# Induced attention into a channel mix on one core: follow-up operations a step later, the gate a step earlier, and two squares in twelve on VectorE

## The chip, the core and the metric

The kernel runs on one core of one Trainium2 chip. TensorE (PE) multiplies matrices into PSUM, VectorE (DVE), ScalarE (ACT) and GpSimd (POOL) work element by element, SyncE (SP) issues the DMAs; each takes its instructions in program order and waits on the others' semaphores. The time is device microseconds of one execution.

## What is computed

The reference, cut to what matters; the four batches have 12608 tokens of 128 channels, there are 32 inducing points, and the hidden width is 1024.

```python
def mab(q, kv):
    s = scale * (q @ kv.transpose(0, 2, 1))
    a = np.exp(s - s.max(-1, keepdims=True))
    a /= a.sum(-1, keepdims=True) + 1e-09
    return a @ kv
h = mab(I, x)            # stage A: 32 points attend to all tokens
y = mab(x, h)            # stage B: every token attends to the 32 rows of h
y_prev = shift(y, 1)     # the token before
xk = mu_k * y + (1 - mu_k) * y_prev
xr = mu_r * y + (1 - mu_r) * y_prev
k = np.maximum(xk @ w_k, 0.0)
v = k * k @ w_v
out = sigmoid(xr @ w_r) * v
```

## The kernel before

**Folding.** Since y = a @ h, the kernel never makes y: it multiplies h into the weights (`combine`, once for each batch) and keeps for each group of 512 tokens a tile `R` with the transposed weights `a`, as a high part (`ah`) and a low part (`al`), both in a float32 form that PE takes at full rate.

**The main loop.** A batch has 25 groups (24 of 512 tokens, one of 320), a group four *units* of 256 hidden columns: 100 units a batch, 400 in all, one for each *step* n of the loop at L998. A step issues, in this order:

- `up` of unit n: four matmuls (L773, L775) into a PSUM tile `ps_a`, of which there are two;
- whatever was handed to `soon(n, ...)`;
- `square` of unit n: `k_t = max(ps_a, 0)` on DVE (L785), `kh = k_t²`, the high part, on ACT (L786), `k_t = k_t²` on ACT in place (L787), then on POOL `kl = k_t - kh` (L789); `k_t`, `kh`, `kl` have four buffers each;
- in one unit of each group, `zgate`: two matmuls (L762, L763) into the group's PSUM tile `ps_v` and the sigmoid on ACT into `rT` (L765);
- for a group finished five steps earlier, `gate` on DVE (`oT = ps_v * rT`, L805; steps with n mod 4 = 0), and a step later `store` (a transpose into `ot` on DVE, L816, and after every fourth group four DMAs on SP, L823);
- `down` of unit n-4: six matmuls (L800) that add into `ps_v`; the first overwrites the gate's logits, so it waits for the sigmoid;
- whatever was handed to `at(n, ...)`, in the order in which it was handed over.

`ps_v` has two buffers, so `zgate` of group g writes where group g-2 was, which `gate` of that group reads in step 4g.

**Segments.** Stage A of the next batch and stage B of this one run inside the loop, one block of 2048 tokens of each for every 12 steps (`SEG`, L976). Below, *position* p is the step's place in its segment, 0 to 11; a unit's number in its group is p mod 4. There are six segments a batch; the fourth batch has no stage A. Then follow `combine` and the first block of stage B of the next batch. In the first batch all begins at step 4.

What the segment begun at s issues, by position (a stage A block goes on into the next segment):

| position | stage A | stage B |
|---|---|---|
| 11, 0, 1, 3 | `btr`: transposes to `xs` (L333), four DMAs each | |
| 1 | | `scores` into PSUM bank `pb_b` (L610) |
| 2, 3 | | transpose, maximum (L617, L620); `sub` (L623) |
| 4 | `expo` of the block before (L393, L394) | `expo` (L627) |
| 5 | `etrans` of the block before (L405) | |
| 6, 7 | `hmm`: products with `e` (L426) | sums (L631); `mult`, `back` (L638, L644) |
| 8 | `acc` | `high`: `ah` out of `pb_b` on ACT (L650) |
| 9 | `scores` into bank `pb_a`, maximum (L361, L364) | `low`: `al` out of `pb_b` on DVE (L654) |
| 10 | `common`: one product into bank `pb_b` (L371) | `spread` of a group: four DMAs into `R` (L664) |
| 11 | `running`: the new maximum (L377 to L382) | `spread`, and so on until position 1 |

Each of the banks `pb_a` and `pb_b` is one buffer: who writes it next waits for its last reader. The last full block of a batch takes the 320 tokens of the tail with it (`t_tr`, `t_scores`, `t_etrans`), which shifts `common` and `running` by a step. `halo` copies the last column of one `R` into the next. `xs` has three buffers, `ot` one.

Of the kernel before, what the change touches and what calls it, by code (L numbers as in the profile page):

```python
# [12 lines left out]
AF = mybir.ActivationFunctionType  # L13
ALU = mybir.AluOpType
# [5 lines left out]
def kernel(  # L20
# [11 lines left out]
    nc = tc.nc  # L32
# [13 lines left out]
    NU = FC // UC  # L46
# [16 lines left out]
    def pb_tile(bank=None):  # L63

        return pb.tile([P, G], F32, name="pb_" + (bank or next(banks)))
# [248 lines left out]
    def stage_a(b, j, at, t):  # L314
# [8 lines left out]
        tail = j == NBLK - 2  # L323
# [122 lines left out]
            at(t + (-1, 0, 1, 3)[c], lambda c=c: btr(c))  # L446
        if tail:
            at(t + 5, t_tr)
            at(t + 10, t_scores)
        at(t + 9, scores)  # L450
        at(t + 10 + tail, common)
        at(t + 11 + tail, running)
        at(t + 16, expo)
        at(t + 17, etrans)
        if tail:
            at(t + 17, t_etrans)
# [5 lines left out]
        k = order_a.index((b, j))  # L462
# [119 lines left out]
    def halo(S, g, far=True):  # L582

        if g == 0:
            nc.vector.memset(S.R[g].bitcast(F32)[:, 0:1], 0.0)
        elif far:
            nc.sync.dma_start(out=S.R[g].bitcast(F32)[:, 0:1], in_=S.R[g - 1].bitcast(F32)[:, G:G + 1])
        else:
            nc.vector.tensor_copy(out=S.R[g][:, 0:1], in_=S.R[g - 1].bitcast(F32)[:, G:G + 1])


    def stage_b(b, j, at, t):

        S = batches[b]
        full = j < NBLK - 1
        L = {}
        if full:
            w = G  # L600
        else:
            w = (TAIL // Q + 31) // 32 * 32
            offs = [min(i * w, TAIL - w) for i in range(Q)]
        nk = w // 32

        def scores():
            ps = L["ps"] = pb_tile("b")
            for i in range(Q):
                rhs = S.xt[j, i] if full else S.xt_tail[:, offs[i]:offs[i] + w]
                nc.tensor.matmul(out=ps[M * i:M * (i + 1), :w], lhsT=S.hT, rhs=rhs,  # L610
                                 start=True, stop=True)
            for i in range(Q):
                S.xt.pop((j, i))

        def trans():
            L["s2"] = st.tile([P, Q * Q, M], F32, name="s2")[:, :nk, :]
            nc.vector.transpose(out=L["s2"].rearrange("p k m -> p (k m)"), in_=L["ps"][:, :w])  # L617

        def maxi():
            nc.vector.tensor_reduce(out=L["ps"][:, :nk], in_=L["s2"], op=ALU.max, axis=AX.X)  # L620

        def sub():
            nc.vector.tensor_tensor(out=L["s2"], in0=L["s2"], op=ALU.subtract,  # L623
                                    in1=L["ps"][:, :nk].unsqueeze(2).broadcast_to([P, nk, M]))

        def expo():
            nc.scalar.activation(out=L["s2"], in_=L["s2"], func=AF.Exp, scale=scale)  # L627

        def total():
            L["sm"] = sm.tile([P, Q * Q, 2], F32, name="sm3", bufs=1)[:, :nk, 0]  # L630
            nc.vector.tensor_reduce(out=L["sm"], in_=L["s2"], op=ALU.add, axis=AX.X)  # L631
            nc.vector.tensor_scalar(out=L["sm"], in0=L["sm"], scalar1=EPS, scalar2=None, op0=ALU.add)

        def recip():
            nc.vector.reciprocal(out=L["ps"][:, :nk], in_=L["sm"])

        def mult():
            nc.vector.tensor_tensor(out=L["s2"], in0=L["s2"], op=ALU.mult,  # L638
                                    in1=L["ps"][:, :nk].unsqueeze(2).broadcast_to([P, nk, M]))

        def back():
            L["aT"] = L["ps"][:, :w]
            if full and b > 0:
                nc.vector.transpose(out=L["aT"].rearrange("p (q s) -> p s q", q=M), in_=L["s2"])  # L644
            else:
                nc.vector.transpose(out=L["aT"], in_=L["s2"].rearrange("p k m -> p (k m)"))

        def high():
            L["ah"] = st.tile([P, G], F32R, name="ah")[:, :w]
            nc.scalar.copy(out=L["ah"], in_=L["aT"])  # L650

        def low():
            L["al"] = st.tile([P, G], F32R, name="al")[:, :w]
            nc.vector.tensor_tensor(out=L["al"], in0=L["aT"], in1=L["ah"].bitcast(F32), op=ALU.subtract)  # L654

        def spread(i):
            src = (L["ah"].bitcast(F32), L["al"].bitcast(F32))
            if full or i == 0:
                S.R[j * Q + i] = r_pool.tile([P, G + 1], F32R, name="R")
                halo(S, j * Q + i)  # L660
            R = S.R[j * Q + (i if full else 0)].bitcast(F32)
            o, lo = (0, 0) if full else (offs[i], i * w - offs[i])
            for q in range(Q):
                nc.sync.dma_start(out=R[M * q:M * (q + 1), 1 + o + lo:1 + o + w],  # L664
                                  in_=src[q % 2][M * i:M * (i + 1), lo:w])

        at(t, scores)
        at(t + 1, trans)
        at(t + 1, maxi)
        at(t + 2, sub)  # L670
        at(t + 3, expo)
        at(t + 5, total)
        at(t + 5, recip)
        at(t + 6, mult)
        at(t + 6, back)
        at(t + 7, high)
        at(t + 8, low)
        for i in range(Q):
            at(t + 9 + i, lambda i=i: spread(i))

    def stage_b_head(gs):

# [64 lines left out]
    class Group:  # L747
# [28 lines left out]
                                 start=False, stop=True)  # L776
            self.ps = ps

        def square(self, u):

            w = self.w
            k = mp.tile([P, UC * G], F32, name="k_t", bufs=4).rearrange("p (c t) -> p c t", c=UC)[:, :, :w]
            kh = mp.tile([P, UC, G], F32R, name="kh", bufs=4)[:, :, :w]
            kl = mp.tile([P, UC, G], F32R, name="kl", bufs=4)[:, :, :w]
            nc.vector.tensor_scalar(out=k, in0=self.ps[:, :, :w], scalar1=0.0, scalar2=None, op0=ALU.max)  # L785
            nc.scalar.activation(out=kh, in_=k, func=AF.Square)  # L786
            nc.scalar.activation(out=k, in_=k, func=AF.Square)  # L787
            self.h[u] = (kh, kl)
            return lambda eng, a, z: eng.tensor_tensor(out=kl[:, :, a:z], in0=k[:, :, a:z],  # L789
                                                       in1=kh.bitcast(F32)[:, :, a:z], op=ALU.subtract)  # L790
# [39 lines left out]
    def run(th):  # L830
        for f in th:
            f()
# [99 lines left out]
    def at(n, f):  # L932
        events.setdefault(n, []).append(f)

    def soon(n, f):
        early.setdefault(n, []).append(f)
# [37 lines left out]
        at(4, lambda: units[0][0].zgate(first=True))  # L974

    SEG = 12  # L976
    for b in range(B):
        t = b * UB + (4 if b == 0 else 0)
        for j in range(NBLK - 1):
            s = t + SEG * j  # L980
            if b + 1 < B:
                stage_a(b + 1, j, at, s)
            stage_b(b, j + 1, at, s + 1)
        if b + 1 < B:
            s = t + SEG * (NBLK - 1)
            combine(b + 1, at, s)
            stage_b(b + 1, 0, at, s + 13)
    units = []
    for b in range(B):
        for g in range(NG):  # L990
            grp = Group(b, g)
# [3 lines left out]
    with tc.manual_schedule():  # L995
        head()
        start()
        for n in range(len(units) + LAG + 2):  # L998
            grp, u = units[n] if n < len(units) else (None, n % NU)
            old, ou = units[n - LAG] if LAG <= n < len(units) + LAG else (None, 0)  # L1000
            if grp is None:
                run(late)
                late = []
            else:
                grp.up(u)
                run(early.pop(n, []))
                low = grp.square(u)
                run(late)
                late = []
                part = grp.w - (grp.w // 2 if n >= len(units) - 3 else 0)  # L1010
                low(nc.gpsimd, 0, part)
                if part < grp.w:
                    late = [lambda low=low, a=part, z=grp.w: low(nc.vector, a, z)]
                if n == end:
                    run(late)
                    late = []
                if n >= NU and u == 2:
                    grp.zgate()
                if u == NU - 2 and n + 2 < len(units):
                    nxt = units[n + 2][0]  # L1020
                    if nxt.b == 0 and nxt.g < Q:
                        halo(nxt.S, nxt.g, far=False)
            m = n - LAG - 1
            if 0 <= m < len(units) and units[m][1] == NU - 1:
                units[m][0].gate()
            if 1 <= m <= len(units) and units[m - 1][1] == NU - 1:
                units[m - 1][0].store()
            if old is not None:
                old.down(ou)
            run(events.pop(n, []))  # L1030
# [30 lines left out]
```

## Time and profile before

| | us |
|---|---|
| median of 3 runs | 1231.35 (1230.76 to 1233.29) |
| the profiled execution | 1226.32 |
| its span, first to last instruction | 1224.5 |
| from the first step to 361.0 (batch 1) | 305.5, PE busy 280.1 |
| 361.0 to 663.0 (batch 2) | 302.0, PE busy 285.5 |
| 663.0 to 955.0 (batch 3) | 292.0, PE busy 274.6 |
| 955.0 to the end (batch 4, no stage A) | 269.5, PE busy 253.3 |

A row of the timeline has the start in microseconds from the span's start, the duration, the engine, the line, the operation, the tiles as out<-in, the shape, and how many instructions were merged; in brackets stands the idle time of the engine before it and what ended that. A row of the waits has the waiting engine and line, what it waited for, the sum, the number of times and the longest. A matmul's duration overlaps the next one's start, so the distance of two starts is what counts.

### The profile page before, as it was taken

Reading aid. Unit: us, or ns where it says so; the run is one execution under the profiler, and the core shown is the slowest. Engines: PE = TensorE matmul, PEld = TensorE weight load, DVE = VectorE, ACT = ScalarE, POOL = GpSimd, SP = SyncE. Lnnn points to the kernel's source line nnn. Section 1 sums busy time; section 2 is a strip of 40 time slices with the busy share of each in tenths; the row PEclk is TensorE's granted clock in tenths of the full one; section 3 lists DMA queues with packets and bytes.
Section 4 is the critical chain, followed back from the end, with each engine's and each line's share of the span. In section 5 each row is a group of like instructions: output and inputs, shape, how many; then the busy total and the mean of one; then the engine's idle time right before and its main releaser. Section 6 shows DMA issues by size and latency. Waiting matters only on the chain.

```text
span 1224.5 us, 17466 instructions
## 1 busy us (share of the span) xinstructions
PE 1132.5 (92%) x5746; PEld 848.7 (69%) x5746; DVE 875.1 (71%) x1211; ACT 1030.6 (84%) x1155; POOL 949.0 (78%) x413
## 2 busy tenths in 40 slices
PE   7779999899999999998999999999899999999998
PEld 5456676667677666776678666667677777777786
DVE  5777777776777787776677777687676766766665
ACT  5478898888888888887888888898888888888996
POOL 1168877787778878886788887788778888888997
PEclk9989999999999999999999999999999999999999
DMA  9112554533326455454035353563232313322222
GB/s 277 44 45 70 128 112 104 115 96 68 51 48 128 115 116 97 107 127 97 2 76 95 99 111 101 125 126 78 40 49 53 57 28 68 70 51 54 40 37 39
DMA packets 273515, 102.30 MB, mean 84 GB/s; under 512 B 232817, under 2 KB 248337, under 8 KB 271121
## 3 DMA queue, kind: packets, MB, share of 16 engines
q1 hardware_dynamic: 273088, 101.17, 38.6%
q8 instruction: 46, 0.75, 0.3%
q14 instruction: 45, 0.36, 0.1%
q10 hardware_dynamic: 336, 0.02, 0.0%
HBM read 28.07 MB, written 25.82 MB: 44 GB/s over the span
## 4 chain that ended last, share of the span: by engine, by line
PE 66%; ACT 16%; DVE 7%; issue 5%; DMA 3%; SPq 2%; POOL 0%; DVEq 0%; ACTq 0%; POOLq 0%
PE ps_v L800 34%; PE ps_a L773 12%; PE ps_a L775 11%; ACT kh L786 5%; ACT k_t L787 3%; DVE k_t L785 3%; ACT L765 2%; PE pb_b L610 2%; PE ps_v L762 1%; PE ps_v L763 1%; PE pb_a L361 1%; ACT L393 1%; ACT rT L765 1%; ACT e1t L394 1%; DMA out_dram<-ot 1%
## 5 line engine op out<-in xcount | busy, mean ns | idle before, releaser
L789 POOL TENSOR_TENSOR kl<-k_t,kh 128x1024 fp32r<-128x1024 f32 (+2 forms) x400 | 940.3, 2367 | 228.0 <-ACT k_t L787 168.8
L785 DVE TENSOR_SCALAR k_t<-ps_a 128x1024 f32<-128x1024 f32 (+1 forms) x400 | 480.7, 1202 | 262.0 <-PE ps_a L775 243.8
L786 ACT ACTIVATE kh<-k_t 128x1024 fp32r<-128x1024 f32 (+1 forms) x400 | 417.6, 1044 | 137.0 <-PE ps_v L800 86.5
L787 ACT ACTIVATE k_t<-k_t 128x1024 f32<-128x1024 f32 (+1 forms) x400 | 419.3, 1048 | 12.7
L773 PE MATMUL ps_a<-R,W 128*128 128x512 f32 (+1 forms) x800 | 333.3, 417 | 0.7 <-ACT R L738 0.7
L775 PE MATMUL ps_a<-R,W 128*128 128x512 f32 (+1 forms) x800 | 319.5, 400 | 0.0
L800 PE MATMUL ps_v<-kh,wvh 128*128 128x512 f32 (+1 forms) x800 | 256.0, 402 | 31.3 <-ACT rT L765 31.3
L800 PE MATMUL ps_v<-kh,wvl 128*128 128x512 f32 (+1 forms) x800 | 252.2, 397 | 0.0
L800 PE MATMUL ps_v<-kl,wvh 128*128 128x512 f32 (+1 forms) x800 | 250.7, 395 | 0.0
L773 PEld LDWEIGHTS ps_a<-R,W 128*128 128x128 f32 x800 | 154.0, 193 | 75.7 <-issue 21.4
L800 PEld LDWEIGHTS ps_v<-kh,wvh 128*128 128x128 f32 x800 | 151.6, 193 | 76.2 <-ACT rT L765 42.6
L800 PEld LDWEIGHTS ps_v<-kh,wvl 128*128 128x128 f32 x800 | 153.1, 192 | 35.6
L775 PEld LDWEIGHTS ps_a<-R,W 128*128 128x128 f32 x800 | 154.7, 193 | 30.7
L800 PEld LDWEIGHTS ps_v<-kl,wvh 128*128 128x128 f32 x800 | 151.3, 190 | 35.1
L816 DVE STREAM_TRANSPOSE ot<-oT 128x512 f32<-128x512 f32 x96 | 67.2, 700 | 12.9 <-DMA out_dram<-ot 12.9
L805 DVE TENSOR_TENSOR oT<-ps_v,rT 128x512 f32<-128x512 f32 (+1 forms) x100 | 67.0, 670 | 0.6 <-PE ps_v L800 0.6
L765 ACT ACTIVATE rT<-ps_v 128x512 f32<-128x512 f32 (+1 forms) x99 | 57.2, 578 | 0.3
L333 DVE STREAM_TRANSPOSE xs<-xb 128x512 f32<-128x512 f32 x72 | 50.0, 694 | 3.1 <-DMA xt<-xs 2.6
L765 ACT ACT_TABLE_LOAD x31 | 39.8, 1283 | 0.6
L762 PE MATMUL ps_v<-R,W 128*128 128x512 f32 (+1 forms) x99 | 39.4, 398 | 0.0
L763 PE MATMUL ps_v<-R,W 128*128 128x512 f32 (+1 forms) x99 | 39.3, 397 | 0.0
L426 PE MATMUL pb_a<-xb,e 128*32 128x128 f32 x576 | 23.3, 279 | 11.7 <-DVE e L405 11.6
(193 smaller groups left out, 613.9 us busy)
## 6 DMA issues: line engine op xcount, KB each, us to landing
out_dram<-ot SPq DMA_DIRECT2D x92, 256.0 KB, 4.4
xb<-in_x_dram SPq DMA_DIRECT2D x18, 1024.0 KB, 5.1
xt<-xs SPq DMA_DIRECT2D x288, 64.0 KB, 2.0
R<-ah SPq DMA_DIRECT2D x184, 64.0 KB, 2.0
R<-al SPq DMA_DIRECT2D x184, 64.0 KB, 2.0
kh<-in_x_dram SPq DMA_DIRECT2D x4, 512.0 KB, 8.0
kl<-in_x_dram SPq DMA_DIRECT2D x4, 512.0 KB, 7.5
xb<-in_x_dram SPq DMA_DIRECT2D x8, 256.0 KB, 5.6
```

The costliest lines, as they stand in the source:

```text
L762: nc.tensor.matmul(out=ps[:, :w], lhsT=S.W[0][:, F:WF], rhs=R[:, 1:w + 1], start=True, stop=False)
L763: nc.tensor.matmul(out=ps[:, :w], lhsT=S.W[1][:, F:WF], rhs=R[:, 0:w], start=False, stop=True)
L765: nc.scalar.activation(out=self.rT, in_=ps[:, :w], func=AF.Sigmoid)
L773: nc.tensor.matmul(out=ps[:, c, :w], lhsT=S.W[0][:, cs], rhs=R[:, 1:w + 1], start=True, stop=False)
L775: nc.tensor.matmul(out=ps[:, c, :w], lhsT=S.W[1][:, cs], rhs=R[:, 0:w], start=False, stop=True)
L785: nc.vector.tensor_scalar(out=k, in0=self.ps[:, :, :w], scalar1=0.0, scalar2=None, op0=ALU.max)
L786: nc.scalar.activation(out=kh, in_=k, func=AF.Square)
L787: nc.scalar.activation(out=k, in_=k, func=AF.Square)
L789: return lambda eng, a, z: eng.tensor_tensor(out=kl[:, :, a:z], in0=k[:, :, a:z], in1=kh.bitcast(F32)[:, :, a:z], op=ALU.subtract)
L800: nc.tensor.matmul(out=self.v, lhsT=wt[:, fc, :], rhs=kk[:, c, :], start=(fc == 0 and n == 0), stop=(fc == FC - 1 and n == 2))
L805: nc.vector.tensor_tensor(out=self.oT, in0=self.v, in1=self.rT, op=ALU.mult)
L816: nc.vector.transpose(out=ot[:, o:o + w], in_=self.oT)
```

## The change

`kh` of the units at positions 4 and 10 is made on DVE, out of PSUM, right behind `k_t`. `low` and the four `spread`s of stage B come a step later. `common`, and the tail's `t_scores`, go from the end of step t+10 to the next step, behind its `up`. Stage A's `expo` comes a step earlier (position 3 of the next segment) with `etrans` where it was. `zgate` is issued with unit 1 of its group and not with unit 2, at positions 1, 5 and 9.

```diff
         if tail:
             at(t + 5, t_tr)
-            at(t + 10, t_scores)
+            soon(t + 11, t_scores)
         at(t + 9, scores)
-        at(t + 10 + tail, common)
+        soon(t + 11 + tail, common)
         at(t + 11 + tail, running)
-        at(t + 16, expo)
+        at(t + 15, expo)
         at(t + 17, etrans)
...
         at(t + 7, high)
-        at(t + 8, low)
+        at(t + 9, low)
         for i in range(Q):
-            at(t + 9 + i, lambda i=i: spread(i))
+            at(t + 10 + i, lambda i=i: spread(i))
...
-        def square(self, u):
+        def square(self, u, on_vector):
...
             nc.vector.tensor_scalar(out=k, in0=self.ps[:, :, :w], scalar1=0.0, scalar2=None, op0=ALU.max)
-            nc.scalar.activation(out=kh, in_=k, func=AF.Square)
+            if on_vector:
+                nc.vector.scalar_tensor_tensor(out=kh, in0=self.ps[:, :, :w], scalar=0.0, in1=k,
+                                               op0=ALU.max, op1=ALU.mult)
+            else:
+                nc.scalar.activation(out=kh, in_=k, func=AF.Square)
             nc.scalar.activation(out=k, in_=k, func=AF.Square)
...
     SEG = 12
+    high_vector = set()
...
             s = t + SEG * j
+            high_vector |= {s + 4, s + 10}
...
-                low = grp.square(u)
+                low = grp.square(u, n in high_vector)
...
-                if n >= NU and u == 2:
+                if n >= NU and u == 1:
                     grp.zgate()
```

Stage B is issued with t = s + 1, so its t + 9 is position 10.

## The prediction

> **What bounds the kernel now.** I read the engines' busy times first, then PE's rows in the waits, then the timeline of one ordinary segment, step by step.
>
> ```profile
> PE 1132.5 (92%) x5746; PEld 848.7 (69%) x5746; DVE 875.1 (71%) x1211; ACT 1030.6 (84%) x1155; POOL 949.0 (78%) x413
> PE ps_v L800 <- ACT rT L765: 31.3, 24, 2.2
> PE pb_a L426 <- DVE e L405: 11.6, 8, 3.3
> PE pb_b L409 <- ACT s L398: 7.6, 3, 2.5
> PE pb_a L341 <- ACT e1t L394: 6.6, 3, 2.2
> DVE ot L816 <- DMA out_dram<-ot: 12.9, 4, 4.8
> ```
>
> PE is the bound. It stands still for few things, all of which end in something late on ACT: the sigmoid, or one of stage A's exponentials (the first, second, third and fourth PE row). An ordinary step of ten matmuls takes 2.34 us (in the rows further down, starts at 807.35 and 809.70).
>
> ```profile
> 808.64 1.06 ACT L787 ACTIVATE k_t<-k_t 128x1024 f32<-128x1024 f32 x1
> 812.06 1.28 ACT L393 ACT_TABLE_LOAD   x1
> 814.22 0.62 ACT L627 ACTIVATE s<-s 128x512 f32<-128x512 f32 x1
> 818.93 1.28 ACT L765 ACT_TABLE_LOAD   x1
> 820.23 0.60 ACT L765 ACTIVATE rT<-ps_v 128x512 f32<-128x512 f32 x1
> 819.57 0.40 PE L775 MATMUL ps_a<-R,W 128*128 128x512 f32 x1
> 820.88 0.73 PE L800 MATMUL ps_v<-kh,wvh 128*128 128x512 f32 x2 [0.91 <-ACT rT L765]
> 271.15 0.63 PE L773 MATMUL ps_a<-R,W 128*128 128x512 f32 x1
> 351.84 0.73 PE L800 MATMUL ps_v<-kh,wvh 128*128 128x512 f32 x2 [2.10 <-ACT rT L765]
> 1073.55 0.63 PE L773 MATMUL ps_a<-R,W 128*128 128x512 f32 x1
> 1073.97 0.63 PE L775 MATMUL ps_a<-R,W 128*128 128x512 f32 x1
> 1077.28 0.40 PE L773 MATMUL ps_a<-R,W 128*128 128x512 f32 x1
> 1106.04 0.73 PE L800 MATMUL ps_v<-kh,wvh 128*128 128x512 f32 x2 [1.80 <-ACT rT L765]
> ```
>
> Behind the exponentials of position 4 ACT still has the squares of units 5 and 6 and a table load before the sigmoid of position 6, which ends at 820.83; at position 8 `down` needs it. The matmul of 820.88 could have started 0.23 behind that of 819.57: 1.08 late, and its pair takes 0.73 where others take 0.63. So 0.91 us shown as idle cost 1.18: to each wait of PE I add 0.27.
>
> The long waits cost twice: from 1073.55, behind a wait of 1.77, matmuls start 0.43 apart, and the step takes 3.73 and not 2.34. Such a slow stretch follows ten of the eleven waits for the sigmoid of 1.77 and above (the first at 351.84, the last at 1106.04) and none of the short ones like that of 820.88. I charge 1.4 each.
>
> [...]
>
> **What goes.** (a) The sigmoid. `zgate` at position 5 puts it ahead of the squares of unit 6; stage A's exponentials (2.16 us, from the table load at 812.06 to 814.22) are a step earlier, and unit 4's `kh` is gone from ACT. I follow ACT through: the squares of unit 3 end at 809.7 (808.64 + 1.06) and, shifted by the 0.17 of (e), near 809.9, stage A's exponentials at 812.0, the in-place square of unit 4 at 813.1, stage B's at 813.6, unit 5's squares at 815.8, load and sigmoid at 817.7; `down` wants it at 819.8. It is over, with 2 us to spare: 31.3 + 24 x 0.27 + 10 x 1.4 = 51.8 us.
>
> (b) The tail's `t_tr` waits at position 5 for stage A's exponential to free `pb_a`; that is now done a step before: 6.6 + 3 x 0.27 + 1.4 for each of two slow stretches (in the first, 0.63 at 271.15) = 10.2.
>
> (c) `t_etrans` waits for the tail's exponential, in the same way: 7.6 + 0.8 = 8.4.
>
> (d) `hmm` waits for `e`: 11.6 + 8 x 0.27 = 13.8. Where the exponential is late, it goes; where `ot` waits for its DMA (four times), `e` is behind that on DVE. SP's queue has one `spread` less ahead of the output's DMAs, but begins the `spread`s nearly 3 us later, so that wait shrinks by some 1.6 of 3.2 us each. I count 9, between 0 and 13.8. Together **79.4 us** go.
>
> **What comes.** First the new DVE instruction, which the trace doesn't show.
>
> ```profile
> L805 DVE TENSOR_TENSOR oT<-ps_v,rT 128x512 f32<-128x512 f32 x96 | 65.1, 678 | 0.0
> L785 DVE TENSOR_SCALAR k_t<-ps_a 128x1024 f32<-128x1024 f32 x384 | 467.6, 1218 | 247.7 <-PE ps_a L775 229.5 <-POOL kl L789 18.0
> L785 DVE TENSOR_SCALAR k_t<-ps_a 128x640 f32<-128x640 f32 x16 | 13.2, 823 | 14.3 <-PE ps_a L775 14.3
> L370 DVE TENSOR_TENSOR mx<-mx,mx 128x1 f32<-128x1 f32 x3 | 4.8, 1592 | 0.0
> ```
>
> It reads PSUM and SBUF like L805. From 640 to 1024 elements a DVE instruction grows by 1.03 ns an element, so 0.678 + 512 x 0.00103 = 1.20 us. Below, 1.0 would be that rate with hardly any fixed part; above, 2.6, if it were held up as the one-element L370 is, whose inputs are both in SBUF. I take 1.20, from L805, which is the nearest.
>
> ```profile
> 805.31 0.69 DVE L620 TENSOR_REDUCE pb_b<-s 128x16 f32<-128x512 f32 x1
> 807.35 0.40 PE L773 MATMUL ps_a<-R,W 128*128 128x512 f32 x1
> 808.00 0.65 DVE L623 TENSOR_TENSOR s<-s,pb_b 128x512 f32<-128x512 f32 x1
> 808.57 1.22 DVE L785 TENSOR_SCALAR k_t<-ps_a 128x1024 f32<-128x1024 f32 x1
> 809.70 0.40 PE L773 MATMUL ps_a<-R,W 128*128 128x512 f32 x1
> 809.71 0.68 DVE L805 TENSOR_TENSOR oT<-ps_v,rT 128x512 f32<-128x512 f32 x1
> 810.64 0.63 PE L800 MATMUL ps_v<-kh,wvh 128*128 128x512 f32 x2
> ```
>
> (e) Position 5: `zgate` behind `gate` behind `kh`. Unit 4's `k_t` ends at 809.79; `kh` starts at 809.82; the next DVE instruction follows 1.14 behind the start of such a one (808.57 to 809.71), so `gate` runs from 810.96 to 811.64. It frees the `ps_v` that `zgate` now wants at 810.64. With 0.05 for the signal (820.83 to 820.88) PE is 1.05 late. DVE comes to position 4 some 0.17 later than before, because step 2 loses `zgate`'s two matmuls (0.47) and L617, L620 then reach past the next `up`; in the fourth batch, without `btr`, it catches up again, and with the tail's small block too. So 15 x (1.22 + 0.10) + 9 x (1.05 + 0.10) = 30.2. Queued behind it on PE is `down`, and through it all else. As idle time this is about 1.05, below the 1.77 of the slow stretches.
>
> At positions 0 and 8 `gate` has no `kh` before it and ends near the point where `zgate` wants it; I charge nothing there, at most 0.4 each.
>
> ```profile
> 790.91 0.50 PE L773 MATMUL ps_a<-R,W 128*128 128x512 f32 x1
> 791.12 0.69 DVE L364 TENSOR_REDUCE mx<-pb_a 128x1 f32<-128x512 f32 x1 [0.59 <-PE pb_a L361]
> 791.73 0.68 DVE L654 TENSOR_TENSOR al<-pb_b,ah 128x512 fp32r<-128x512 f32 x1
> 793.81 0.38 PE L371 MATMUL pb_b<-ident,mx 128*128 128x128 f32 x2
> 794.96 0.63 PE L800 MATMUL ps_v<-kh,wvh 128*128 128x512 f32 x2
> ```
>
> (f) Position 11: `common` behind `low`. Both use `pb_b`. Now `low` ends at 792.41, `common` starts at 793.81: nothing waits. After, `k_t` of unit 10 starts 1.21 behind its `up` at 792.12, `kh` at 793.36, `low` at 794.50, to 795.18. `common` stands behind unit 11's `up`: 0.61 earlier than 794.96, as `zgate` and `common` have left step 10, hence 794.35. It is 0.88 late with the signal, 0.98 with the restart: 15 x 0.98, and 3 x 0.5 for the tail's `t_scores` behind a small `low`: 16.2. DVE's `running` follows without harm. What `common` itself waited for (the tail's 1.6 us behind L370) stays as it is, a step later.
>
> ```profile
> 106.39 0.58 SPq L664 DMA_DIRECT2D R<-al  x1
> 109.09 0.40 PE L773 MATMUL ps_a<-R,W 128*128 128x512 f32 x1
> R<-al SPq DMA_DIRECT2D x184, 64.0 KB, 2.0
> 358.22 0.58 SPq L664 DMA_DIRECT2D R<-al  x1
> 361.13 0.40 PE L773 MATMUL ps_a<-R,W 128*128 128x512 f32 x1
> ```
>
> (g) `spread` is late twice, in the first batch, whose stages begin four steps later. Step 16 (109.09) reads the `R` whose last DMA is issued at 106.39 and lands 2.0 later. `low` behind `kh` ends 2.8 later, so that lands at 111.2, while the step would start at 109.7: 1.5. Step 100 (361.13): `low` is 2.2 later, lands at 362.4: 1.3. With restarts 3.0. Elsewhere a group has five steps or more.
>
> `kh` leaving ACT (48 x 1.06 us) is worth nothing more by itself: ACT is off the path once (a) is gone. `kl` still ends steps before `down` asks for it.
>
> The sum: 79.4 - 30.2 - 16.2 - 3.0 = **30.0 us** less. Against the profiled execution's own 1226.3 (its span 1224.5 and 1.8 around it) that is 1196.3; the median of the runs is 5.0 above that execution, so 1201.4 there.
>
> **The rivals.** *The new waits are not there*, or half of them, because something I take as ordered isn't, or DVE is earlier than I think. For it: DVE is busy 71% only. Against it: both waits come from instructions in program order and buffers with one or two copies, and (b) shows that PE does wait for a bank's last reader. Half of (e) and (f) gone gives 1178, all 1155.
>
> *The new wait crosses into the slow clock*, the case on the other side. Place: `zgate` at position 5. If `kh` on DVE takes 1.9 and not 1.2, the idle time there comes to 1.77, where the slow stretches begin, and each of 24 costs 0.7 + 1.4, each of 18 `common`s 0.7: 63 us, hence 1264. Each 0.1 us more costs 4.2; at about 0.7 all that is won is gone, just where the clock adds its share. For it: L370. Against it: L805, L623 and L654 with one input in PSUM, which nothing holds up.
>
> *SP becomes late*: the `spread`s begin later and pile up with `btr`, so outputs issued at position 5 land after the next `store` wants `ot`. The price is at most what that wait is now, 12.9, once more: 1214.
>
> *The sigmoid stays late*: the squares of unit 5 wait for DVE behind `gate`. If half of (a) remains: 1227, hardly a change.
>
> *The slow stretches have another cause* and stay, ten in (a) and two in (b): 1201 + 12 x 1.4 = 1218. Against it: each begins within some 2 us of a long wait's end.
>
> **How the numbers follow.** Forecast 0.56 (its own range 1188 to 1216: `kh` between 1.0 and 1.4 is 8 either way, (d) 5 to 9); waits half or wholly missing 0.13; SP late 0.12; sigmoid late 0.07; slow clock 0.09; slow stretches with another cause 0.03. The range takes in the half-missing waits at one end and the sigmoid at the other: 1176 to 1229. A measurement of this kernel tells a change from about 0.2%, 2.5 us: faster 0.84, same 0.05, slower 0.11, with the sigmoid's 0.07 split between the last two.
>
> **What would show it.** In the profile after, L800's wait for L765 should be nearly gone from PE's rows, with L341 and L409. In its place L762 should wait for DVE's `gate` 24 times at about 1.05 us idle, L371 for DVE's `low` 15 times at 0.7. `kh` on DVE should last 1.20. Step 8 of the fourth batch's segments should take 2.4 and step 9 be without the 0.43 spacing. I am wrong if PE's idle time isn't in those two places, or if slow stretches follow position 5.

## The result, and the profile after

| | before | after |
|---|---|---|
| median of four runs, us | 1231.05 (1228.02 to 1233.29) | 1221.39 (1219.53 to 1221.54) |
| the profiled execution | 1226.32 | 1221.54 |
| its span | 1224.5 | 1219.7 |

The ratio is 0.992, with a 95% interval of 0.9896 to 0.9943: 9.7 us or 0.8% less, a third of the forecast's 30.0. The forecast was summed against the profiled execution, and by the two profiled executions the gain is only 4.8.

The busy times (from the page) and the waits of the kernel after; a row of the waits has the sum, the number of times and the longest:

```profile
PE 1123.6 (92%) x5746; PEld 832.9 (68%) x5746; DVE 964.6 (79%) x1259; ACT 978.6 (80%) x1107; POOL 950.3 (78%) x413
PE ps_v L762 <- DVE oT L809: 41.2, 38, 2.0
PE pb_b L371 <- DVE al L654: 14.7, 15, 1.0
PE ps_a L773 <- DMA R<-al: 3.2, 2, 1.8
PE pb_b L349 <- DVE al L654: 2.7, 3, 1.2
PE pb_b L371 <- DVE mx L370: 2.1, 3, 0.7
DVE ot L820 <- DMA out_dram<-ot: 5.9, 6, 2.2
```

Lines below the edit have moved: `down` is now L804, `gate` L809, `store` L820, `kl` L793; `kh` is L787 on DVE. PE no longer waits for the sigmoid (before 31.3 us, 24 times), for `e` (11.6, 8) or for stage A's exponentials (7.6 and 6.6). Two large rows have come instead, both of them waits for DVE: `zgate` for `gate` and `common` for `low`. 89 us of work went to DVE or grew there (875.1 to 964.6), 52 left ACT.

The waits sorted by position, from PE's timeline, with 0.27 for each restart and 1.4 for each slow stretch as in the prediction:

| term | forecast, us | trace after, us |
|---|---|---|
| (a), (b), (c) sigmoid and exponentials | -70.4 | -70.4 (no such row is left) |
| (d) `hmm` for `e` | -9 | -13.8 and a slow stretch, -1.4 = -15.2 |
| `common` for L370 (4.8 to 2.1) | 0 | -2.7 |
| (e) `zgate` at position 5 | +30.2 | 27.9 idle + 24 x 0.27 = +34.4 |
| (f) `common` and `t_scores` | +16.2 | 17.4 idle + 18 x 0.27 = +22.3 |
| (g) `spread` late | +3.0 | 3.2 + 2 x 0.27 + 1.4 = +5.1 |
| `zgate` at position 9 | 0 | 11.4 idle + 9 x 0.27 = +13.8 |
| `zgate` at position 1, three of the five in `combine` | 0 | 1.9 idle + 5 x 0.27 = +3.3 |
| a slow stretch behind a `zgate` | 0 | +1.4 |
| first step later (55.57 to 57.07) | 0 | +1.5 |
| sum | -30.0 | -6.5; measured -4.8 |

The costs that were named are there, each somewhat larger. The large row that was priced at nothing is position 9: 13.8 us. There `zgate` follows `gate` of position 8, which has no `kh` in front of it. What makes it late is seen by going back along DVE in the timeline. First the kernel before, positions 6 and 7 of a segment in the fourth batch:

```profile
1061.70 4.79 POOL L789 TENSOR_TENSOR kl<-k_t,kh 128x1024 fp32r<-128x1024 f32 x2 [0.37 <-ACT k_t L787]
1068.03 2.40 POOL L789 TENSOR_TENSOR kl<-k_t,kh 128x1024 fp32r<-128x1024 f32 x1 [1.54 <-ACT k_t L787]
1066.25 0.68 DVE L631 TENSOR_REDUCE sm<-s 128x16 f32<-128x512 f32 x1
1066.96 0.18 DVE L632 TENSOR_SCALAR sm<-sm 128x16 f32<-128x16 f32 x1
```

L632, which adds the epsilon to 16 sums a partition, starts at 1066.96, when GpSimd is idle (1066.49 to 1068.03), and lasts 0.18. The timeline of the kernel after, in the same segment:

```profile
1064.61 2.42 POOL L793 TENSOR_TENSOR kl<-k_t,kh 128x1024 fp32r<-128x1024 f32 x1 [1.64 <-ACT k_t L791]
1065.01 2.05 DVE L632 TENSOR_SCALAR sm<-sm 128x16 f32<-128x16 f32 x1
1067.09 0.26 DVE L635 RECIPROCAL pb_b<-sm 128x16 f32<-128x16 f32 x1
1067.26 1.21 DVE L785 TENSOR_SCALAR k_t<-ps_a 128x1024 f32<-128x1024 f32 x1
1068.38 0.67 DVE L638 TENSOR_TENSOR s<-s,pb_b 128x512 f32<-128x512 f32 x1
1069.09 0.73 DVE L644 STREAM_TRANSPOSE pb_b<-s 128x512 f32<-128x512 f32 x1
1069.72 1.20 DVE L785 TENSOR_SCALAR k_t<-ps_a 128x1024 f32<-128x1024 f32 x1
1070.85 0.67 DVE L809 TENSOR_TENSOR oT<-ps_v,rT 128x512 f32<-128x512 f32 x1
1071.57 0.50 PE L762 MATMUL ps_v<-R,W 128*128 128x512 f32 x1 [1.52 <-DVE oT L809]
```

L632 starts 0.40 behind the start of a `kl` and ends at 1067.06, 0.03 behind that `kl`'s end (1067.03). Behind it DVE has no pause up to `gate`, and `zgate` waits 1.52 us for that. It is so nearly every time: after, L632 runs into a `kl` in 24 of its 27 executions (23 of the shape shown, 4 of the tail's). The groups of DVE by line and shape, with busy time and mean ns, first before, then after:

```profile
L632 DVE TENSOR_SCALAR sm<-sm 128x16 f32<-128x16 f32 x23 | 4.4, 190 | 0.8
```

```profile
L632 DVE TENSOR_SCALAR sm<-sm 128x16 f32<-128x16 f32 x23 | 30.3, 1317 | 0.8
L787 DVE SCALAR_TENSOR_TENSOR kh<-ps_a,k_t 128x1024 fp32r<-128x1024 f32 x48 | 58.8, 1225 | 5.0
```

The same 23 instructions take 26 us more. The new `kh` itself takes 1.225. The trace of before had the case already, in four of the 27 executions (0.48 to 1.54 us, each ending 0.03 behind a `kl`); the shortest of them, with the `kl` that ends at 488.69:

```profile
486.29 2.40 POOL L789 TENSOR_TENSOR kl<-k_t,kh 128x1024 fp32r<-128x1024 f32 x1 [2.39 <-ACT k_t L787]
488.25 0.48 DVE L632 TENSOR_SCALAR sm<-sm 128x16 f32<-128x16 f32 x1
```

### The profile page after: what moved, and what is told of

Read it like the earlier page. It is cut to its first block, busy times and chain, and to the rows that moved or that the text cites. A ratio compares the mean times of both kernels' runs of the same rounds, so it can differ in the third digit from the quotient of the medians.

```text
span 1219.7 us, 17555 instructions
## 1 busy us (share of the span) xinstructions
PE 1123.6 (92%) x5746; PEld 832.9 (68%) x5746; DVE 964.6 (79%) x1259; ACT 978.6 (80%) x1107; POOL 950.3 (78%) x413
## 4 chain that ended last, share of the span: by engine, by line
PE 63%; DVE 21%; issue 5%; DMA 4%; SPq 4%; ACT 2%; DVEq 0%; ACTq 0%
PE ps_v L804 32%; PE ps_a L773 11%; PE ps_a L775 10%; DVE k_t L785 8%; PE ps_v L762 2%; DMA out_dram<-ot 2%; DVE oT L809 2%; PE ps_v L763 2%; PE pb_a L426 2%; DVE kh L787 2%; PE pb_b L610 1%; SPq L664 1%; DVE sm L632 1%; SPq L336 1%; PE pb_a L361 1%
## 5 line engine op out<-in xcount | busy, mean ns | idle before, releaser
L793 POOL TENSOR_TENSOR kl<-k_t,kh 128x1024 fp32r<-128x1024 f32 (+2 forms) x400 | 941.6, 2371 | 220.4 <-ACT k_t L791 191.4
L790 ACT ACTIVATE kh<-k_t 128x1024 fp32r<-128x1024 f32 (+1 forms) x352 | 366.9, 1042 | 119.3 <-PE ps_v L804 71.9
L773 PE MATMUL ps_a<-R,W 128*128 128x512 f32 (+1 forms) x800 | 326.8, 409 | 4.1 <-DMA R<-al 3.2
L775 PE MATMUL ps_a<-R,W 128*128 128x512 f32 (+1 forms) x800 | 314.3, 393 | 0.0
L804 PE MATMUL ps_v<-kh,wvh 128*128 128x512 f32 (+1 forms) x800 | 250.7, 395 | 0.1
L804 PE MATMUL ps_v<-kh,wvl 128*128 128x512 f32 (+1 forms) x800 | 249.0, 392 | 0.0
L804 PE MATMUL ps_v<-kl,wvh 128*128 128x512 f32 (+1 forms) x800 | 249.0, 392 | 0.0
L773 PEld LDWEIGHTS ps_a<-R,W 128*128 128x128 f32 x800 | 151.5, 189 | 81.1 <-issue 42.0
L804 PEld LDWEIGHTS ps_v<-kh,wvl 128*128 128x128 f32 x800 | 150.2, 189 | 34.4
L804 PEld LDWEIGHTS ps_v<-kl,wvh 128*128 128x128 f32 x800 | 150.1, 188 | 34.5
L775 PEld LDWEIGHTS ps_a<-R,W 128*128 128x128 f32 x800 | 151.4, 189 | 30.3
L804 PEld LDWEIGHTS ps_v<-kh,wvh 128*128 128x128 f32 x800 | 148.5, 189 | 33.5 <-ACT rT L765 0.8
L762 PE MATMUL ps_v<-R,W 128*128 128x512 f32 (+1 forms) x99 | 42.9, 433 | 41.2 <-DVE oT L809 41.2
L820 DVE STREAM_TRANSPOSE ot<-oT 128x512 f32<-128x512 f32 x96 | 67.2, 700 | 6.8 <-DMA out_dram<-ot 5.9
L809 DVE TENSOR_TENSOR oT<-ps_v,rT 128x512 f32<-128x512 f32 (+1 forms) x100 | 67.0, 670 | 0.5 <-PE ps_v L804 0.5
L787 DVE SCALAR_TENSOR_TENSOR kh<-ps_a,k_t 128x1024 fp32r<-128x1024 f32 x48 | 58.8, 1225 | 5.0
L762 PEld LDWEIGHTS ps_v<-R,W 128*128 128x128 f32 x99 | 18.5, 187 | 63.3 <-DVE oT L809 58.3
```

The lines of the kernel that those rows point to most:

```text
L762: nc.tensor.matmul(out=ps[:, :w], lhsT=S.W[0][:, F:WF], rhs=R[:, 1:w + 1], start=True, stop=False)
L773: nc.tensor.matmul(out=ps[:, c, :w], lhsT=S.W[0][:, cs], rhs=R[:, 1:w + 1], start=True, stop=False)
L775: nc.tensor.matmul(out=ps[:, c, :w], lhsT=S.W[1][:, cs], rhs=R[:, 0:w], start=False, stop=True)
L787: nc.vector.scalar_tensor_tensor(out=kh, in0=self.ps[:, :, :w], scalar=0.0, in1=k, op0=ALU.max, op1=ALU.mult)
L804: nc.tensor.matmul(out=self.v, lhsT=wt[:, fc, :], rhs=kk[:, c, :], start=(fc == 0 and n == 0), stop=(fc == FC - 1 and n == 2))
L809: nc.vector.tensor_tensor(out=self.oT, in0=self.v, in1=self.rT, op=ALU.mult)
```

## The experiments

Two theories follow from this reading. **The `kl`**: L632, which works from SBUF to SBUF, is held up until a `kl` that is running has ended (0.18 us in a pause of GpSimd, 2.05 beside a `kl`), and the change moved it from the pause into the `kl`; that makes position 9. **The queue**, its rival: DVE has 58.8 us more to do, and position 9 is late for that, whatever L632 takes. A second question is what each part of the change is worth. In the experiments each ratio is to the kernel before, timed beside it on the same chip (medians there 1228.9, 1227.8 and 1228.2, and 1231.05 beside the changed kernel), with its 95% interval. A difference between times of different experiments is thus good to some 3 us.

### 1. After, with the small sum in PSUM

```diff
-            nc.vector.tensor_scalar(out=L["sm"], in0=L["sm"], scalar1=EPS, ...)
+            nc.vector.tensor_scalar(out=L["ps"][:, :nk], in0=L["sm"], scalar1=EPS, ...)
...
-            nc.vector.reciprocal(out=L["ps"][:, :nk], in_=L["sm"])
+            nc.vector.reciprocal(out=L["ps"][:, :nk], in_=L["ps"][:, :nk])
```

> The changed kernel, with the small sum of stage B (one addition over 128x16, at position 6) written to PSUM and not to SBUF; all else as it is. [...] Then the addition takes about 0.2 us, the wait of 1.5 us at position 9 goes in the fourth batch and in each batch's first segment, and the kernel takes about 1209 us. Rival: DVE simply has more to do since it makes two high parts, and is late at position 8 for that; then the addition may get shorter but the wait at position 9 stays, 1219 to 1222 us.

1207.17 us, 0.9819 (0.9799 to 0.984): 14.2 less than after, 12.4 by the two ratios. The group of L632 and PE's first wait:

```profile
L632 DVE TENSOR_SCALAR pb_b<-sm 128x16 f32<-128x16 f32 x23 | 4.1, 178 | 0.8
PE ps_v L762 <- DVE oT L809: 30.1, 29, 2.3
```

L632 is back at 0.18 us (0.165 to 0.179 in all 27 executions), also where a `kl` is running (at 1055.25, beside the one from 1054.83 to 1057.25); the nine waits at position 9 are gone, those at position 5 stay, and a fourth-batch segment takes 31.87 in place of 33.6. DVE's work is the same but for the held-up time, so the queue alone doesn't make position 9. Why L632 ends 0.03 us behind a `kl` with its output in SBUF and takes 0.18 beside one with its output in PSUM, no run shows.

### 2. After, with `gate` ahead of the square

```diff
+                m = n - LAG - 1
+                if m >= 0 and units[m][1] == NU - 1:
+                    units[m][0].gate()
                 low = grp.square(u, n in high_vector)
```

`gate` keeps its later place only in steps without an `up`.

> The changed kernel, with the gate's multiplication issued ahead of the step's squares, so ahead of the high part on DVE. Theory: all 38 waits of the gate's matmuls for it go (41.2 us idle, some 51 with the restarts), about 1172 us, up to 1185 where something else is late next. Rival: the product that the gate reads is itself late, or the relu behind it now is, so that up waits for PSUM: 1205 us or more.

1187.28 us, 0.9668 (0.964 to 0.9696). PE's waits:

```profile
PE pb_b L371 <- DVE al L654: 16.9, 15, 2.1
PE ps_v L804 <- ACT rT L765: 5.3, 8, 1.2
PE ps_v L762 <- DVE oT L809: 0.4, 1, 0.4
```

With `gate` no longer behind `k_t` and `kh`, `zgate` waits once, for 0.4, so (e) is as the prediction had it. Of 41.2 + 38 x 0.27 = 51.5 the kernel gains 34.1: the sigmoid is waited for again (5.3 us), and PE waits somewhat longer for `low` (16.9 for 14.7, two of the waits now 2.0 and 2.1). The rest was not followed up.

### 3. After, without the high parts on VectorE

```diff
-                low = grp.square(u, n in high_vector)
+                low = grp.square(u, False)
```

> The changed kernel with no high part on VectorE; the order of everything else as changed. Theory: the high parts on DVE cause the waits at positions 5 and 11 (24 of 1.35 us and 18 of about 1.1), and ACT, with two squares more in 12 steps, still has the sigmoid done in time: about 1172 us. The long addition stays, so the wait at position 9 stays in part. Rival: ACT needed the relief, the sigmoid is late again at position 8 by 1 us or more: 1200 us or more.

1166.6 us, 0.9493 (0.9471 to 0.9516). PE's first wait, and the group of L632:

```profile
PE ps_v L762 <- DVE oT L809: 7.5, 10, 1.6
L632 DVE TENSOR_SCALAR sm<-sm 128x16 f32<-128x16 f32 x23 | 15.5, 675 | 0.8
```

The two squares in twelve cost 54.8 us (1221.4 - 1166.6; 52.5 by the ratios), and the rest of the change gains about 62. The sigmoid isn't late although ACT has its 48 squares back: moving `zgate` and `expo` is enough for that, as run 7 shows too (0.3 us of waits left in each). The waits at positions 5 and 11 go with the high parts, as (e) and (f) had it: 24 and 15 of them became two each. Position 9 is theirs as well for the most part: in five of the six segments of the fourth batch L632 is not held up any more (0.17 to 0.18 us), and of nine waits at position 9 two are left, both where it lasts over 2 us.

### 4. After, with `common` at the end of its step

```diff
-        soon(t + 11 + tail, common)
-        at(t + 11 + tail, running)
+        at(t + 11 + tail, common)
+        at(t + 12 + tail, running)
```

> The changed kernel with the product for the common maximum at the end of step 11 and the running maximum a step later. Theory: the 15 waits for the low part on the bank (14.7 us idle, 18.7 with restarts) go, and nothing else is late for it: about 1203 us. Rival: DVE is as late a step on, or the running maximum then delays stage A's exponential and its followers: 1215 us or more.

1215.42 us, 0.9888 (0.9864 to 0.9912). The 15 waits of 0.98 are gone, an ordinary segment goes from 36.13 to 34.88, 1.25 x 15 = 18.8 us. Only 6 of it arrive, 4 by the ratios; the waits of PE and DVE:

```profile
PE pb_b L371 <- DVE mx L370: 6.5, 3, 2.7
PE pb_b L349 <- DVE al L654: 4.1, 3, 2.6
DVE ot L820 <- DMA out_dram<-ot: 9.8, 5, 3.6
```

The rest is lost again mostly in the tail's block: there PE waits longer for DVE ahead of `common` and `t_scores` (the two rows were 4.8 us in the kernel after and are 10.6, with slow stretches behind two of the waits of 2.6 to 2.7), and the output's DMAs are waited for more. So (f) is where it was put, and of what this repair wins it gives back most.

### 5 to 7. Before, with the moves alone and together

```diff
-        at(t + 16, expo)
+        at(t + 15, expo)
```

```diff
-                if n >= NU and u == 2:
+                if n >= NU and u == 1:
                     grp.zgate()
```

The first alone:

> The kernel before with only stage A's exponential a step earlier (position 3). Theory: the waits for that exponential go (some 10 us at the bank, 8 at the tail's transpose, part of the 14 before the products with e), and the sigmoid is no longer late in segments with both stages, but still late in the fourth batch, with the slow stretches there (about 20 us): 1185 to 1195 us. Rival: two steps with exponentials load the table more often, or the sigmoid stays late everywhere: 1205 us or more.

1203.34 us, 0.98 (0.9762 to 0.9839). The waits:

```profile
PE ps_v L800 <- ACT rT L765: 29.7, 23, 2.2
PE pb_a L426 <- DVE e L405: 7.7, 3, 3.4
```

The tail's waits and the short ones for `e` go, those for the sigmoid stay nearly whole (31.3 to 29.7): a step is not enough for them. A miss by 8.

The second alone:

> The kernel before with only the gate's matmuls and sigmoid a step earlier (unit 1). Theory: all waits for the sigmoid go with their slow stretches (52 us), those for stage A's exponential stay, and with no high part on DVE the gate's matmuls wait for little: 1177 to 1187 us. Rival: the gate's matmuls wait for the multiplication of the group two before in any case, 24 times about 1 us: 1200 us or more.

1196.71 us, 0.9737 (0.9707 to 0.9768). The waits:

```profile
PE pb_a L426 <- DVE e L405: 9.7, 9, 3.1
PE ps_v L762 <- DVE oT L805: 9.5, 11, 2.4
DVE ot L816 <- DMA out_dram<-ot: 22.2, 8, 4.6
```

The sigmoid's row falls from 31.3 to 0.3, so `zgate` is what clears (a). But 31 us are gained and not 41 to 51: the rival was right in part, `zgate` waits 9.5 for `gate` (11 times, not 24), and `store` now waits 22.2 for its DMAs and not 12.9, with `e` behind it on DVE.

Both:

> The kernel before with both moves, the exponential and the gate a step earlier, and nothing else of the change. Theory: what the change wins, without the waits that it brings (high parts on DVE, low and spread a step later): 1231 less some 75, so 1150 to 1162 us. It is faster than the changed kernel without high parts on DVE (1166.6) by the late spreads, about 3 us. Rival: the later low and common were needed, and without them the product for the common maximum or the gate waits for DVE: 1170 us or more.

1185.9 us, 0.9651 (0.9621 to 0.9681), where 1150 to 1162 were expected. Of the waits for `e`, 8.3 us are left in three long ones (row with run 12). These two moves are 19 us short of run 3, which has the later `spread`s and `common` as well.

### 8. Before, with both moves, the small sum and the scalings by way of PSUM, and `gate` first

Besides the edits of runs 1, 2, 5 and 6, the four scalings of `h` in `combine` read PSUM:

```diff
-                nc.vector.tensor_scalar(out=h4, in0=h, scalar1=mu, ...)
+                nc.vector.tensor_scalar(out=h4, in0=ps[:, :P], scalar1=mu, ...)
```

> [...] Theory: nothing on PE is left to wait for but the start and the output's DMA; 3 to 8 us less than with both moves alone: 1145 to 1157 us. [...]

1173.4 us, 0.9548 (0.9515 to 0.958): 12.5 less than run 7, more than the 3 to 8 expected, with `zgate` waiting 1.3 for `gate` and not 10.9. It is still a miss by 16, since run 7 itself was 24 above its range: the three waits for `e` are still there (9.8 us) and the output's are 26.9.

### 9 and 10. After, without the high parts, the small sum and the scalings by way of PSUM

The edits of runs 1 and 3 and that of the scalings:

> [...] Theory: against 1166.6 without high parts, the waits of the gate's matmuls that are left (7.5 us idle, 10 times) go in part: 1155 to 1163 us. [...]

1157.51 us, 0.942 (0.9379 to 0.9462), the best of all: 63.9 below after. With `gate` ahead of the square besides:

> As the one before, with the gate's multiplication ahead of the step's squares. Theory: the last waits for it go, but the relu stands behind it, so squares and sigmoid come 0.6 us later and some waits for the sigmoid come back: within 4 us of the one before either way. Rival: the waits for the gate were a real loss: 5 us less or more.

1159.39 us, 0.9442 (0.94 to 0.9483), no difference. Run 9's wait for `gate` is down to

```profile
PE ps_v L762 <- DVE oT L809: 2.1, 5, 0.6
```

so little was left for the earlier `gate` to win. With the small sum written to PSUM and the scalings read from it, the kernel without the high parts is 9 us faster (1166.6 - 1157.5). Run 9 also shows what makes `zgate` wait in `combine` (0.52 to 0.54, three times): these waits stay in runs 1 and 3 and are gone here, where the scalings of L519 read PSUM and take 0.34 us each.

### 11. After, with `zgate` back at unit 2

```diff
-                if n >= NU and u == 1:
+                if n >= NU and u == 2:
```

> The changed kernel with only the gate's matmuls put back to unit 2. Theory: the 38 waits behind the gate's multiplication (41 us idle, 51 with restarts) go, since they come from its new place; the sigmoid, now behind the squares of unit 6 again, is late by 0 to 1 us at position 8: 1172 to 1195 us. Rival: the gate's move is what won the sigmoid's 52 us, and they come back in full: 1215 us or more.

1210.63 us, 0.985 (0.9814 to 0.9887), a miss by 16. The 38 waits for `gate` are gone, and

```profile
PE ps_v L804 <- ACT rT L765: 24.7, 14, 2.5
PE pb_b L371 <- DVE al L654: 10.3, 15, 2.0
```

the sigmoid is waited for again, now with nine slow stretches, although ACT has 48 squares less. So with the high parts on DVE, and `gate` behind them, `zgate` has no good place: early it waits for `gate`, late the sigmoid is late.

### 12. Before, with both moves and the later `spread`s

The edits of run 7, and:

```diff
-            at(t + 9 + i, lambda i=i: spread(i))
+            at(t + 10 + i, lambda i=i: spread(i))
```

> The kernel before with both moves (1185.9) and only the spreads' DMAs a step later; low and common as before. Theory: the later spreads let the output's DMAs go first on SP, DVE waits less for the output tile, and long stalls with their slow stretches at positions 6 and 7 and in the fourth batch go: 1166 to 1176 us. Rival: the order on SP doesn't matter, or it is the late low and common that helped: 1183 us or more.

1170.81 us, 0.9532 (0.9497 to 0.9568). The waits of run 7, then of this one:

```profile
PE 1127.9 (95%) x5746; PEld 839.0 (71%) x5746; DVE 888.6 (75%) x1211; ACT 1021.5 (86%) x1155; POOL 946.9 (80%) x413
PE pb_a L426 <- DVE e L405: 8.3, 3, 2.8
DVE ot L816 <- DMA out_dram<-ot: 22.2, 8, 4.4
```

```profile
PE 1119.2 (96%) x5746; PEld 833.8 (71%) x5746; DVE 891.3 (76%) x1211; ACT 1019.9 (87%) x1155; POOL 946.9 (81%) x413
PE pb_a L426 <- DVE e L405: 2.2, 3, 1.3
DVE ot L816 <- DMA out_dram<-ot: 19.8, 7, 3.6
```

The later `spread`s alone are worth 15.1 us. The three waits of `store` that stand ahead of `e` at position 6 fall from 4.2, 4.4 and 4.3 to 2.9, 1.9 and 2.1, while others grow; the waits for `e` fall by 6.1 in all, and PE's busy time by 8.7 with the same 5746 matmuls, as four slow stretches of run 7 (at 232.0, 477.1, 760.9 and 1040.4) are not set off, three of them behind the waits for `e`. The queue of SP shows the reason: ahead of the output's DMAs of the second of these waits stood two `spread`s without a pause in run 7, and one here, and the first of these DMAs is issued 1.30 ahead of the start of step 140 and not 1.24 behind it.

## Why the prediction was right in direction and wrong in size

- **(a), (b), (c)** were right: no wait for the sigmoid or stage A's exponentials is left, and the twelve slow stretches behind them are gone. Run 6 shows that `zgate` clears (a); run 5 that `expo` clears (b) and (c) and hardly touches (a).
- **(d)** was put at 9 of 0 to 13.8; all 13.8 went, and with them a slow stretch that the prediction had not charged (behind 236.53, 1.4). The first reason given, the late exponential, is borne out by run 5, where five of the eight waits go; the second, the wait of `store` behind the `spread`s, by run 12, where it is worth more than the prediction allowed. Of the four waits of `store` only three (4.8, 3.6 and 4.1) stood ahead of `e`; the fourth was 0.3.
- **(e)** was right in place, number and cause (24 waits; runs 2 and 3): 34.4 for 30.2. More than half of the excess is in three first segments of a batch, with idle times of 1.96, 1.99 and 1.36. `kh` took 1.225 us for 1.20; so the rival with a `kh` of 1.9 is out.
- **(f)** was right in place, number and cause (run 3), but too small: 22.3 for 16.2. The timeline of an ordinary segment after, positions 10 and 11:

```profile
464.68 0.49 PE L773 MATMUL ps_a<-R,W 128*128 128x512 f32 x1
465.98 1.23 DVE L785 TENSOR_SCALAR k_t<-ps_a 128x1024 f32<-128x1024 f32 x1 [0.39 <-PE ps_a L775]
467.31 1.23 DVE L787 SCALAR_TENSOR_TENSOR kh<-ps_a,k_t 128x1024 fp32r<-128x1024 f32 x1
468.44 0.68 DVE L654 TENSOR_TENSOR al<-pb_b,ah 128x512 fp32r<-128x512 f32 x1
469.18 0.49 PE L371 MATMUL pb_b<-ident,mx 128*128 128x128 f32 x2 [0.98 <-DVE al L654]
```

  `k_t` starts 1.30 behind the start of `up` and not 1.21 (the first matmul takes 0.33 to the next start), and `kh`, which reads `k_t`, starts 0.10 behind its end and not 0.03: 0.16 of the 0.27 by which each `common` is later than forecast. For the 0.03 the prediction shows no row.
- **(g)** was right in both places; the second of its waits (1.85) set off a slow stretch, so 5.1 for 3.0.
- **The step that failed** is the sentence that at positions 0 and 8 `gate` has no `kh` before it and ends near the point where `zgate` wants it, so "I charge nothing there, at most 0.4 each". At position 9 it cost idle times of 1.5 to 1.7 in seven segments and of 0.2 in two, 13.8 us with the restarts, and 12 to 14 were won when L632 alone was freed (run 1). Of the 25.2 us of gain that are missing by the profiled executions this is the largest part; (e) and (f), put too small, are 10.3. The sum carried DVE's order but let every other DVE instruction keep its duration. The prediction had the warning row in hand: it quoted L370, one element in 1592 ns, "whose inputs are both in SBUF", and weighed it as a bound for `kh` alone, instead of asking which small instructions with operands in SBUF would now meet a `kl`. L632 itself was held up four times before; in the other 23 it met a pause or started ahead of the `kl`, which was luck of timing.
- Not foreseen either, and smaller: `zgate` behind `gate` at position 1 3.3, a slow stretch 1.4, the start 1.5. In `combine` the scalings of L519 stretch as L632 does (`h4k` by `omuk` from a mean of 0.53 to 2.15 us, `h4r` by `mur` from 0.27 to 1.87), and runs 1, 3 and 9 show that the waits there come from them. The start does not come from the change: over all the kernels traced the first step begins between 55.57 and 57.29. 1.7 us of the balance stay open.
- **The median** was put 5.0 above the profiled execution, as before the change; after, the two agree (1221.4 and 1221.5).
- **The range**, 1176 to 1229, holds the measured 1221.4, but by luck: the forecast's own 1188 to 1216 does not, and the part above it was there for a late sigmoid that did not come.

Of the rivals none came about: the new waits are all there, the slow clock doesn't follow position 5 but for once (behind 668.58, a granted clock of 0.62), SP is not late (`store` waits 5.9 and not 12.9), the sigmoid isn't late, and the slow stretches went with the waits. The case that came was not among them: the forecast's mechanism, with a cost that the trace of before could have suggested.

## What to carry to other kernels

Ask of every instruction that an edit shifts not only what it waits for but what it will run beside: a tiny VectorE operation from SBUF to SBUF in front of a critical queue took 0.18 us in a GpSimd pause and 2.05 beside a GpSimd operation, and sending its output to PSUM won 12 to 14 us. An engine that is only 71% busy is no free place when its instructions stand in one queue with the releases of single or double buffers: 48 instructions of 1.2 us cost 53 to 55 us of time. Price the parts of a change separately and distrust their sum, since one part here gained 62 and another lost 53 to 55, and moves taken alone were each taken up in part by the next wait.

## What the runs showed of the hardware

The slow stretches have no sharp bound. Here are three waits of the kernel after, behind which matmuls were or were not spaced 0.43 apart, and one such stretch by window (length, busy times and, behind POOL, the granted clock):

```profile
361.73 0.47 PE L773 MATMUL ps_a<-R,W 128*128 128x512 f32 x1 [1.85 <-DMA R<-al]
377.63 0.50 PE L762 MATMUL ps_v<-R,W 128*128 128x512 f32 x1 [1.96 <-DVE oT L809]
668.58 0.50 PE L762 MATMUL ps_v<-R,W 128*128 128x512 f32 x1 [1.99 <-DVE oT L809]
361.00:364.50 3.50, 2.77 (x10) 2.49 (x11) 1.03 (x1) 1.11 (x2) 3.50 (x3) 0.67 0.37 83
```

Idle times of 1.85 and 1.99 us were followed by a slow stretch (granted clock 0.67 around the first, 0.62 behind the second), those of 1.96 and 1.74 were not (1.00 behind each). In the kernel before, the slow step of 1073.55, 3.73 us long, ran at a granted clock of 0.59. Longer ones were passed over too: before, the three waits of `t_etrans` of 2.5 us had none behind them. The window behind the first of them, with a granted clock of 1.00:

```profile
309.50:313.00 3.50, 3.47 (x29) 2.61 (x29) 2.67 (x5) 2.76 (x3) 1.35 (x1) 1.00 0.02 5
```

So a price of 1.4 us for each wait of 1.8 and above is an upper one, and what decides is not known from these runs.

Of the float32 form of `ah` and `al` the trace of before shows this: a product of 128x512 with `R` takes 0.40 us, and the next one starts 0.24 later (807.35 and 807.59, granted clock 1.00), while one of the same size with both operands in plain float32 (L531, eight times) takes 0.59 at the least.
